# Attention with a gated feed-forward in one kernel: down products in one run per two sections, the activation and the gate reordered, fewer key transfers

## Chip, core and metric

The kernel runs on one core of a Trainium2 chip. The metric is the device time of one execution, in microseconds; the median of the runs is compared. TensorE multiplies matrices (PE in the profile, PEld is its weight load), VectorE is DVE, ScalarE is ACT, GpSimd is POOL, and SyncE (SP) issues the transfers.

## The reference

The input `x` has 2048 tokens of width 576. It is normalized once, and two branches read the result: attention with 32 heads of width 18, and a feed-forward of width 4608 with a gelu gate. The output joins them.

```python
def _A_ref(x, wqkv, wo):
    B, S, D = x.shape
    H = 32
    Dh = D // H
    qkv = (lambda x, *d: x.transpose(*d))((x @ wqkv).reshape(B, S, 3, H, Dh), 2, 0, 3, 1, 4)
    q, k, v = qkv[0], qkv[1], qkv[2]
    scores = jnp.einsum("bhqd,bhkd->bhqk", q, k) * (Dh ** -0.5)
    p = _softmax(scores, axis=-1)
    o = jnp.einsum("bhqk,bhkd->bhqd", p, v)
    return (lambda x, *d: x.transpose(*d))(o, 0, 2, 1, 3).reshape(B, S, D) @ wo

def _B_ref(x, w_gate, w_up, w_down):
    return (_gelu(x @ w_gate) * (x @ w_up)) @ w_down

x = A_x
xn = _layernorm(x, axis=-1)
s = _A_ref(xn, A_wqkv, A_wo)
g = _silu(_B_ref(xn, B_w_gate, B_w_up, B_w_down))
return x + s * g
```

## The kernel before, in words

Values are split into a high and a low part (`hi`, `lo`), and a product is made of three: high by high, high by low, low by high.

The prologue normalizes `x` by blocks of 512 tokens (`norm`), transposes it on TensorE (`transposes`, `pt`), makes queries and keys (`project`, `po`) and values (`values_of`), and stores all of it to DRAM (`qk`, `vs`, and `xhs` for the feed-forward). In the last block `split_wo` loads, splits and stores the output weights.

The main part is a sequence of 144 sections, counted from 0, that mix both branches. Four token blocks have 18 rounds each, and a round has two sections (G = 2). A section makes the gate and up sums `pg` and `pu` of 128 of the 4608 columns for 512 tokens: 27 pairs of products, each pair on the two halves of TensorE's rows. Among these pairs the program puts attention's products (`spread`): pairs of a score product `pe` (whose exponential ACT writes to `pT`) and a product `pm` of a later unit (whose row maximum DVE takes). The first nine sections (`FIRST` says how many pairs each takes) hold only products for maxima, sections 9 to 136 hold scores, the last seven none. After its pairs a section has, in this order, the values of attention (`values`, `acc`), the turn of a row of maxima (`max_end`, every fourth section), a projection by the output weights (`project_o`, `po`, in 8 sections per block, on dates that `at` writes down), and down products (`downs`, `py`). PE runs in program order; a scheduler orders the other engines' instructions, save those under `keep_in_program_order`.

`activate` makes gelu(`pg`) times `pu` from two operations on ACT and three on DVE; `pg` and `pu` have two banks together, so the next section's sums wait for the last reader. `finish` splits the result into `hh` and `hl`, and after a round's second section it splits the down weights `dh`, `dl` and queues the round's down products in two halves: token groups 0 and 1 in the next section, 2 and 3 in the one after. Each half is 24 products in four groups of six, and DVE adds each group to `Y` (it copies in round 0). In the last round of a block `down` then puts silu on `Y` at once, chunk by chunk of 128 by 288 values (`gate`: a tanh on ACT into the one buffer `th`, a DVE operation back into `Y`), and SP stores `Y` to `ys`. There are eight chunks at the end of each of the first three blocks, which falls in sections 36 and 37, 72 and 73, 108 and 109. `load_xy` reads a chunk back when its projection is due.

The banks of PSUM go by tags: `f` two (`pg`, `pu`), `s` two (`pe`, `py`), `m` three (`pm`, `po`), `acc` one. `load_k` and `load_q` fetch the 54 rows of a head (high, low, high for keys) in three transfers each; four heads are loaded for a chunk.

Of the kernel before, what the change touches and what calls it, by code (L numbers as in the profile page):

```python
# [8 lines left out]
F32 = mybir.dt.float32  # L9
# [8 lines left out]
P = 128  # L18
# [21 lines left out]
NF = NB * NR * G  # L40
FIRST = (0, 3, 5, 5, 5, 5, 5, 6, 6)
MROW = 3 * DH
HO = 7
# [8 lines left out]
def f(ap):  # L52
    return ap.bitcast(F32)
# [13 lines left out]
def kernel(ctx: ExitStack, tc: tile.TileContext, x, wqkv, wo, w_gate, w_up, w_down, out):  # L67
# [67 lines left out]
    with tc.tile_pool(name="pro", bufs=1) as pro, tc.tile_pool(name="pps", bufs=1, space=PSUM) as pps:  # L135
# [45 lines left out]
        def norm(xr, b, between=None):  # L181
# [21 lines left out]
            return last  # L203

        def transposes(b, xr):
            xt = XT[b % 2]
            pts = [pps.tile([P, TB], F32, name="pt", bufs=KT + 1) for k in range(KT + 1)]
            for j in range(4):
                for k in range(KT + 1):
                    nc.tensor.transpose(pts[k][:, j * P:(j + 1) * P], xr[j][:, k * P:(k + 1) * P], ident)  # L210
            for k in range(KT + 1):
                split_t(pts[k], k, xt)
            return xt
# [10 lines left out]
        for v in VN:  # L224
            nc.vector.memset(v, 1.0)
        ORDER = (4, 5, 0, 1, 6, 7, 8, 2, 3)
        WQK, WV = {}, {}
# [41 lines left out]
        def split_wo(k):  # L269
            n = min(KO, D - k * KO)  # L270
            raw = raw_tile([KO, D])
            tc.keep_in_program_order(nc.sync.dma_start(raw[0:n], wo[k * KO:k * KO + n, :]))
            hi, lo = (pro.tile([KO, D], F32R, name=f"wo{i}", tag="rawp", bufs=5) for i in range(2))
            split(hi[0:n], lo[0:n], raw[0:n])
            for i, t in enumerate((hi, lo)):
                nc.sync.dma_start(wos[i, k * KO:k * KO + n, :], f(t)[0:n])

# [21 lines left out]
        for b in range(NB):  # L299
            for n, t in enumerate(ORDER):  # L300
# [13 lines left out]
                if b == 0 and n in (7, 8):  # L314
                    split_wv(n - 7, raw_v[n - 7])
                project(b, t, xt)
                if b == NB - 1 and n < NK:
                    split_wo(n)
                if n == 4 and b + 1 < NB:
# [17 lines left out]

    FF = {"w": ahead, "xd": XD, "down": [], "n": 0}
    finals = []
# [16 lines left out]
    def gate(o, th, yy):  # L356

        nc.scalar.activation(th, yy, AF.Tanh, scale=0.5)
        nc.vector.scalar_tensor_tensor(o, th, 1.0, yy, op0=ALU.add, op1=ALU.mult)  # L359

    def activate(pg, pu):
        t1 = ffn.tile([P, TB], F32, name="t1", bufs=1)
        t2 = ffn.tile([P, TB], F32, name="t2", bufs=1)
        nc.scalar.activation(t1, pg, AF.Square)
        nc.vector.scalar_tensor_tensor(t2, t1, 1.0 / GC, pg, op0=ALU.add, op1=ALU.mult)  # L365
        nc.scalar.activation(t1, t2, AF.Tanh, scale=GC * GS)
        nc.vector.scalar_tensor_tensor(t2, t1, 1.0, pg, op0=ALU.add, op1=ALU.mult)
        nc.vector.scalar_tensor_tensor(t1, t2, 0.5, pu, op0=ALU.mult, op1=ALU.mult)  # L368
        return t1

    def down(b, r, hs, wd, Y, js):
# [18 lines left out]
        if b < NB - 1 and r == NR - 1:  # L390
            for j in js:
                t = b * 4 + j
                for c in range(2):
                    yy = Y[:, j, 288 * c:288 * c + 288]
                    gate(yy, ffn.tile([P, 288], F32, name="th"), yy)
                nc.sync.dma_start(ys[t * P:(t + 1) * P, :], Y[:, j, :])

    def section(specials=(), tag="f", raw_d=None, early=None):
# [6 lines left out]
        if g == 0:  # L405
            FF["hs"] = []
            if r == 0:
                FF["Y"] = ffn.tile([P, TB // P, D], F32, name="Y")
        keep = tc.keep_in_program_order if n == NU * NA + len(FIRST) + 1 else lambda i: i
# [22 lines left out]
    def finish(pool=ffn, cut=split, bufs=1):  # L432

        n = FF["n"] - 1
        b, r = divmod(n // G, NR)
        hh = ffn.tile([P, TB], F32R, name="hh", bufs=G + 1)
        hl = ffn.tile([P, TB], F32R, name="hl", bufs=G + 1)
        cut(hh, hl, FF["act"])
        FF["hs"].append((hh, hl))
        if n % G == G - 1:  # L440
            wd = FF.pop("wd", None)
            if not wd:
                wd = [pool.tile([P, G, D], F32R, name=m, bufs=bufs) for m in ("dh", "dl")]
                cut(*wd, FF["rawd"])
            for h in range(2):
                FF["down"].append((b, r, FF["hs"], wd, FF["Y"], (2 * h, 2 * h + 1), n + 1 + h))

# [53 lines left out]
    def project_o(b, i, S2=None, o=None):  # L501
# [10 lines left out]
        if b < NB - 1:  # L512
            nc.vector.scalar_tensor_tensor(yy, yy, 0.5, po[:, 0:288], op0=ALU.mult, op1=ALU.mult)
            nc.gpsimd.tensor_tensor(yy, yy, xx, op=ALU.add)
# [20 lines left out]
    for b in range(NB):  # L535
        last = b == NB - 1
        for k in range(NK):
            t0 = b * AB + max(-(-min(H, (k + 1) * HO) // QD) * NA + 3, 2 * NA + 10 + 3 * k)
            if not (last and k == NK - 1):
                at(t0, 0, load_o, b, k)  # L540
                at(t0 + 2 - last, 2, norm_o, k)
        first = (b + 1) * AB + 1 if last else max((b + 1) * AB + 6, (b + 1) * NR * G - len(FIRST) + 3)
        at(first - 2, 0, load_wo, 0)
        at(first - 1, 2, split_o, 0)
        for i in range(GROUPS):
            n = first + i
            if last and n >= ENDS - 1:
# [11 lines left out]
    with tc.tile_pool(name="att", bufs=1, reuse_waits="tile") as att:  # L559
# [7 lines left out]

        def load_k(n, keep=lambda i: i):

# [3 lines left out]
            cols = slice(c * TB, (c + 1) * TB)  # L573
            for r in range(2):
# [16 lines left out]

        def load_q(u):
            j, g = divmod(u, NQ)
            cols = slice(j * TB, (j + 1) * TB)
            for r in range(2):
                t = QS[u, r] = att.tile([P, TB], F32R, name=f"q{r}", bufs=3)
                for a in range(2):
                    q = f(t)[64 * a:64 * a + MROW, :]
                    h = QD * g + 2 * r + a
                    rows = slice(h * DH, (h + 1) * DH)  # L600
                    for n, i in enumerate((0, 0, 1)):
                        nc.sync.dma_start(q[n * DH:(n + 1) * DH, :], qk[i, rows, cols])

# [121 lines left out]
        for n in range(NU * NA):  # L725
# [22 lines left out]
    with tc.tile_pool(name="epi", bufs=1, reuse_waits="tile") as epi:  # L748
# [40 lines left out]
        for Y, j, c in finals:  # L789
# [6 lines left out]
            else:  # L796
                nc.vector.scalar_tensor_tensor(ss, th, 0.5, ss, op0=ALU.mult, op1=ALU.mult)
                put(ss, j, cc, nc.gpsimd)
        for i, o in zip(range(HIND + 1, GROUPS), os):
            th, ss, j, cc = late[i]  # L800
            po = project_o(NB - 1, i, o=o)
            nc.vector.scalar_tensor_tensor(ss, th, 0.5, po, op0=ALU.mult, op1=ALU.mult)
            put(ss, j, cc, nc.vector)
# [28 lines left out]
```

## Time and profile before

| | |
|---|---|
| median of 3 runs | 2670.77 us (2667.56 to 2672.83) |
| the profiled execution | 2674.07 us, of which the program's span is 2672.3 us |
| PE busy | 2648.8 us, 99% of the span |
| DVE busy | 2007.3 us, 75% |
| ACT busy | 1440.9 us, 54% |
| POOL busy | 1354.0 us, 51% |
| exponentials (`pT`, 128x512) | 2048, of 600 ns |
| row maxima (`mx`, 128x512) | 2048, of 686 ns |
| down products (`py`, 288 columns) | 3456, of 294 to 310 ns, overlapping |
| adds to `Y` (128x288) | 544, of 457 ns |
| the tanh of the gate (128x288) | 24 of 447 ns, and 8 in the last block |
| DMA | 121 GB/s on the mean, 44.8% of the 16 engines' time |

Products overlap in the pipeline, so a product's duration is longer than its step; what counts is the distance from one start to the next. A line of the timeline gives the start in the span, the time, engine, source line and operation, the tiles written and read, the shape and the count; in brackets stands the engine's idle time ahead of it and what ended it. Section numbers are counted on PE's products, and a section starts with its first `pg`.

### The profile page before, as it was taken

The page shows a single profiled execution, that of the slowest core. Times are in us where ns is not written, and L with a number is a line of the kernel's source. Part 1 is how long each engine was busy: PE and PEld are TensorE (multiplying, and loading weights), DVE is VectorE, ACT ScalarE, POOL GpSimd, SP SyncE. Part 2 cuts the span into 40 slices and gives each one's busy share as a digit, 9 for nine tenths or more (in the row PEclk, how much of TensorE's full clock was granted, in tenths as well). Part 3 has the DMA queues.
Part 4 walks back from the last instruction along what each step waited for, and adds up shares of the span by engine and source line. Part 5 has one row for each costly group of instructions (what it writes and reads, how often), then busy time and mean ns, then how long its engine had stood idle before and what let it go on. Part 6 is the DMA issues. An engine that isn't in the chain of part 4 may idle for free.

```text
span 2672.3 us, 55506 instructions
## 1 busy us (share of the span) xinstructions
PE 2648.8 (99%) x21000; PEld 2025.0 (76%) x21000; DVE 2007.3 (75%) x3432; ACT 1440.9 (54%) x2553; POOL 1354.0 (51%) x1439
## 2 busy tenths in 40 slices
PE   8999999999999999999999999999999999999999
PEld 7887777777777777777777777777777777777777
DVE  5327888888888877788888877788888877888445
ACT  3222466555666555566556655555666554666532
POOL 2117544544465555544456555554445556444563
PEclk9999999999999999999999999999999999999999
DMA  8866433344354334543346335433345454433341
GB/s 254 264 229 155 114 96 96 94 103 105 103 141 122 97 103 117 142 105 102 98 106 161 100 99 141 123 103 99 100 106 119 126 140 126 115 101 92 77 111 56
DMA packets 389143, 323.64 MB, mean 121 GB/s; under 512 B 105544, under 2 KB 302664, under 8 KB 388876
## 3 DMA queue, kind: packets, MB, share of 16 engines
q1 hardware_dynamic: 388876, 320.08, 44.8%
q8 instruction: 167, 2.74, 0.4%
q14 instruction: 100, 0.82, 0.1%
HBM read 266.58 MB, written 52.85 MB: 120 GB/s over the span
## 4 chain that ended last, share of the span: by engine, by line
PE 96%; DVE 2%; DMA 0%; ACT 0%; issue 0%; POOL 0%; SPq 0%; DVEq 0%
PE pg L351 27%; PE acc L673 17%; PE py L381 17%; PE pe L639 10%; PE pm L612 9%; PE pu L351 7%; PE po L156 7%; PE po L511 2%; DVE mx L613 1%; PE pt L210 0%; DVE Y L387 0%; DVE t L365 0%; DVE Y L359 0%; PE pm L622 0%; DMA xx<-in_A_x_dram 0%
## 5 line engine op out<-in xcount | busy, mean ns | idle before, releaser
L640 ACT ACTIVATE pT<-pe 128x512 f32<-128x512 f32 x2048 | 1165.3, 600 | 767.4 <-PE pm L612 610.7
L613 DVE TENSOR_REDUCE mx<-pm 128x1 f32<-128x512 f32 x2048 | 1295.2, 686 | 49.8 <-PE pm L612 29.2
L351 PE MATMUL pg<-xd,wh 64*128 64x512 f32 x2592 | 948.6, 398 | 0.5 <-issue 0.5
L351 PE MATMUL pu<-xd,wh 64*128 64x512 f32 x2592 | 946.5, 397 | 0.0
L639 PE MATMUL pe<-q,KS 56*128 56x512 f32 x2048 | 818.1, 407 | 0.1
L612 PE MATMUL pm<-KS,q 54*128 54x512 f32 x2048 | 799.5, 394 | 3.5 <-DVE mx L613 1.9
L91 POOL TENSOR_SCALAR wh<-raw 128x384 fp32r<-128x384 f32 x432 | 222.2, 515 | 882.6 <-DMA raw<-in_B_w_up_dram 516.0
L351 PEld LDWEIGHTS pg<-xd,wh 64*128 64x128 f32 x2592 | 483.3, 187 | 58.0 <-issue 22.6
L351 PE MATMUL pg<-xd,wl 64*128 64x512 f32 x1296 | 507.6, 392 | 0.0
L351 PE MATMUL pu<-xd,wl 64*128 64x512 f32 x1296 | 507.1, 391 | 0.0
L351 PEld LDWEIGHTS pu<-xd,wh 64*128 64x128 f32 x2592 | 483.6, 187 | 9.3 <-DVE t L368 1.4
L673 PE MATMUL acc<-pT,VS 128*32 128x512 f32 x4096 | 466.0, 595 | 0.0
L92 POOL TENSOR_TENSOR wl<-raw,wh 128x384 fp32r<-128x384 f32 x432 | 437.8, 1014 | 34.5
L639 PEld LDWEIGHTS pe<-q,KS 56*128 56x128 f32 x2048 | 369.3, 184 | 82.8 <-ACT pT L640 23.4
L612 PEld LDWEIGHTS pm<-KS,q 54*128 54x128 f32 x2048 | 377.2, 184 | 38.0 <-DVE mx L613 6.4
L387 DVE TENSOR_TENSOR Y<-py,Y 128x288 f32<-128x288 f32 x544 | 248.2, 457 | 203.5 <-PE py L381 202.6
L381 PE MATMUL py<-dh,hh 128*128 128x288 f32 x1152 | 357.6, 310 | 2.3 <-DVE Y L387 1.3
L381 PE MATMUL py<-dl,hh 128*128 128x288 f32 x1152 | 339.8, 295 | 0.0
L381 PE MATMUL py<-dh,hl 128*128 128x288 f32 x1152 | 338.5, 294 | 0.0
L673 PEld LDWEIGHTS acc<-pT,VS 128*32 128x32 f32 x4096 | 120.4, 109 | 275.8 <-issue 264.5
L381 PEld LDWEIGHTS py<-dh,hh 128*128 128x128 f32 x1152 | 216.0, 187 | 81.1 <-issue 41.1
L351 PEld LDWEIGHTS pg<-xd,wl 64*128 64x128 f32 x1296 | 242.1, 187 | 20.0
(110 smaller groups left out, 2811.6 us busy)
## 6 DMA issues: line engine op xcount, KB each, us to landing
KS<-qk SPq DMA_DIRECT2D x1536, 36.0 KB
raw<-in_B_w_gate_dram SPq DMA_DIRECT2D x144, 288.0 KB
raw<-in_B_w_up_dram SPq DMA_DIRECT2D x144, 288.0 KB
raw<-in_B_w_down_dram SPq DMA_DIRECT2D x68, 576.0 KB
VS<-vs SPq DMA_DIRECT2D x128, 152.0 KB
qk<-t SPq DMA_DIRECT2D x72, 256.0 KB
q<-qk SPq DMA_DIRECT2D x384, 36.0 KB
xd<-xhs SPq DMA_DIRECT2D x24, 384.0 KB
```

Source lines behind the costliest of these rows:

```text
L91: first = nc.gpsimd.tensor_scalar(hi, raw, 1.0, 1.0, op0=ALU.mult, op1=ALU.mult)
L92: nc.gpsimd.tensor_tensor(lo, raw, f(hi), op=ALU.subtract)
L156: nc.tensor.matmul(o, st, m, start=(i == 0), stop=(i == len(TERMS) - 1))
L351: nc.tensor.matmul(o, w[1 + wp][k][rr, c, :], xd[xp][k][rr, c, :], start=(i == 0), stop=(i == len(terms) - 1))
L381: nc.tensor.matmul(py, a[:, tt], w[:, g, cc], start=(n == 0), stop=(n == 3 * G - 1))
L387: nc.vector.tensor_tensor(yy, py, yy, op=ALU.add)
L511: nc.tensor.matmul(po[:, 0:288], o[x][0:n, k, :], OW[w][0:n, k, :], start=(m == 0), stop=(m == len(terms) - 1))
L612: nc.tensor.matmul(pm, QS[u, r][rr, t * P:(t + 1) * P], KS[(u * NA + c) % KB][r][rr, :], start=True, stop=True)
L613: nc.vector.tensor_reduce(MX[u][:, 2 * r + a, t, c:c + 1], pm, axis=AX.X, op=ALU.max)
L639: nc.tensor.matmul(pe, KS[(u * NA + c) % KB][r][rr, t * P:(t + 1) * P], QS[u, r][rr, :], start=True, stop=True)
L640: nc.scalar.activation(PT[u, kt][:, 2 * r + a, :], pe, AF.Exp, scale=SCALE)
L673: nc.tensor.matmul(ACC[u][32 * a:32 * a + 32, :], VS[(u * NA + c) % VB][:, v:v + 32], pt[:, a, :], start=(kt == 0), stop=(kt == NT - 1), s ...
```

## The change

`JOIN` names the sections whose rounds have all their down products in the section after the round, 48 in one run; the section after that has none. Projections of the first three blocks are dated two sections apart, in the sections that have the run. `activate` reads `pg` in three operations (square, DVE, a copy on ACT) and `pu` in one, on DVE, before the tanh; the factor 0.5 moves into the gate's scales. Silu of the first three blocks leaves `down`: `gates` runs one section later, with tanh on ACT, two operations on GpSimd and a store for each chunk, and `Y` is one tile for the whole run. 64 idle transposes of the identity are put ahead of the first transposes. Two rows of a head's three are loaded in one transfer, the first keys and queries are loaded by halves, the output weights' stores move two projections back, the lead sections get two empty places at the end, and some dates of `load_o` move.

```diff
+JOIN = (len(FIRST), len(FIRST) + NU * NA - G)
...
+        def warm(n):
+            o = pps.tile([P, TB], F32, name="po", bufs=3)
+            for i in range(n):
+                nc.tensor.transpose(o[:, 0:P], ident, ident)
...
+                if b == 0 and j == 0:
+                    warm(64)
...
+        def store_wo(k, n, hi, lo):
             for i, t in enumerate((hi, lo)):
-                nc.sync.dma_start(wos[i, k * KO:k * KO + n, :], f(t)[0:n])
+                tc.keep_in_program_order(nc.sync.dma_start(wos[i, k * KO:k * KO + n, :], f(t)[0:n]))
...
+                if b == NB - 1 and 2 <= n < NK + 2:
+                    store_wo(*parts.pop(0))
                 if b == NB - 1 and n < NK:
-                    split_wo(n)
+                    parts.append(split_wo(n))
...
     def gate(o, th, yy):
-        nc.scalar.activation(th, yy, AF.Tanh, scale=0.5)
+        nc.scalar.activation(th, yy, AF.Tanh, scale=0.25)
         nc.vector.scalar_tensor_tensor(o, th, 1.0, yy, op0=ALU.add, op1=ALU.mult)
 
     def activate(pg, pu):
         t1 = ffn.tile([P, TB], F32, name="t1", bufs=1)
         t2 = ffn.tile([P, TB], F32, name="t2", bufs=1)
         nc.scalar.activation(t1, pg, AF.Square)
-        nc.vector.scalar_tensor_tensor(t2, t1, 1.0 / GC, pg, op0=ALU.add, op1=ALU.mult)
-        nc.scalar.activation(t1, t2, AF.Tanh, scale=GC * GS)
-        nc.vector.scalar_tensor_tensor(t2, t1, 1.0, pg, op0=ALU.add, op1=ALU.mult)
-        nc.vector.scalar_tensor_tensor(t1, t2, 0.5, pu, op0=ALU.mult, op1=ALU.mult)
+        nc.vector.scalar_tensor_tensor(t1, t1, 1.0 / GC, pg, op0=ALU.add, op1=ALU.mult)
+        nc.scalar.activation(t2, pg, AF.Copy)
+        nc.vector.tensor_tensor(t2, t2, pu, op=ALU.mult)
+        nc.scalar.activation(t1, t1, AF.Tanh, scale=GC * GS)
+        nc.vector.scalar_tensor_tensor(t1, t1, 1.0, t2, op0=ALU.add, op1=ALU.mult)
         return t1
...
         if b < NB - 1 and r == NR - 1:
-            for j in js:
-                t = b * 4 + j
-                for c in range(2):
-                    yy = Y[:, j, 288 * c:288 * c + 288]
-                    gate(yy, ffn.tile([P, 288], F32, name="th"), yy)
-                nc.sync.dma_start(ys[t * P:(t + 1) * P, :], Y[:, j, :])
+            FF["gates"] += [(b, j, c, Y) for j in js for c in range(2)]
+
+    def gates():
+        for k, (b, j, c, Y) in enumerate(FF["gates"]):
+            rows, cc = slice(b * TB + j * P, b * TB + (j + 1) * P), slice(288 * c, 288 * c + 288)
+            if k < 3:
+                th = op.tile([P, 288], F32, name="th", tag=("yy", "yy", "xx")[k], bufs=(2, 2, 1)[k])
+            else:
+                th = ffn.tile([P, 288], F32, name="th")
+            tc.keep_in_program_order(nc.scalar.activation(th, Y[:, j, cc], AF.Tanh, scale=0.25))
+            nc.gpsimd.tensor_scalar(th, th, 1.0, 1.0, op0=ALU.add, op1=ALU.mult)
+            nc.gpsimd.tensor_tensor(th, th, Y[:, j, cc], op=ALU.mult)
+            nc.sync.dma_start(ys[rows, cc], th)
+        FF["gates"] = []
...
-                FF["down"].append((b, r, FF["hs"], wd, FF["Y"], (2 * h, 2 * h + 1), n + 1 + h))
+                once = JOIN[0] <= n < JOIN[1]
+                FF["down"].append((b, r, FF["hs"], wd, FF["Y"], (2 * h, 2 * h + 1), n + 1 + (0 if once else h)))
...
+        if not last:
+            first += (first + len(FIRST)) % G
...
-            n = first + i
+            n = first + i * (1 if last else G)
...
-                    for n_, i in enumerate((0, 1, 0)):
-                        keep(nc.sync.dma_start(kk[n_ * DH:(n_ + 1) * DH, :], qk[i, rows, cols]))
+                    keep(nc.sync.dma_start(kk[0:2 * DH, :], qk[:, rows, cols]))
+                    keep(nc.sync.dma_start(kk[2 * DH:MROW, :], qk[0, rows, cols]))
...
-        load_k(0)
-        load_q(0)
+        for r in range(2):
+            load_k(0, rs=(r,))
+            load_q(0, (r,))
...
-            section([lambda s=s: lead_pair(s) for s in range(slot, slot + m)], "s" if n == 1 else "f", lead_raw)
+            section([lambda s=s: lead_pair(s) for s in range(slot, slot + m)] + (m > 0) * 2 * [lambda: None],
+                    "s" if n == 1 else "f", lead_raw)
...
+            gates()
             tasks(n, 0)
```

More of the change, by code (lines that the diff above doesn't have):

```diff
@@ L225 @@
             nc.vector.memset(v, 1.0)
+        parts = []
         ORDER = (4, 5, 0, 1, 6, 7, 8, 2, 3)
@@ L274, in split_wo @@
             split(hi[0:n], lo[0:n], raw[0:n])
+            return k, n, hi, lo
+        def store_wo(k, n, hi, lo):
             for i, t in enumerate((hi, lo)):
-                nc.sync.dma_start(wos[i, k * KO:k * KO + n, :], f(t)[0:n])
+                tc.keep_in_program_order(nc.sync.dma_start(wos[i, k * KO:k * KO + n, :], f(t)[0:n]))
         NQT = 2 * D // P
@@ L335 @@
     ps = ctx.enter_context(tc.tile_pool(name="ps", bufs=1, space=PSUM))
-    FF = {"w": ahead, "xd": XD, "down": [], "n": 0}
+    FF = {"w": ahead, "xd": XD, "down": [], "gates": [], "n": 0,
+          "Y": ffn.tile([P, TB // P, D], F32, name="Y")}
     finals = []
@@ L406, in section @@
             FF["hs"] = []
-            if r == 0:
-                FF["Y"] = ffn.tile([P, TB // P, D], F32, name="Y")
         keep = tc.keep_in_program_order if n == NU * NA + len(FIRST) + 1 else lambda i: i
@@ L512, in project_o @@
         if b < NB - 1:
-            nc.vector.scalar_tensor_tensor(yy, yy, 0.5, po[:, 0:288], op0=ALU.mult, op1=ALU.mult)
+            nc.vector.scalar_tensor_tensor(yy, yy, 0.25, po[:, 0:288], op0=ALU.mult, op1=ALU.mult)
             nc.gpsimd.tensor_tensor(yy, yy, xx, op=ALU.add)
@@ L537 @@
         for k in range(NK):
-            t0 = b * AB + max(-(-min(H, (k + 1) * HO) // QD) * NA + 3, 2 * NA + 10 + 3 * k)
+            t0 = b * AB + max(-(-min(H, (k + 1) * HO) // QD) * NA + 3, 22 + 3 * k)
             if not (last and k == NK - 1):
@@ L566, with load_k @@
             nc.vector.memset(vv[:, VC * VW:], 0.0)
-        def load_k(n, keep=lambda i: i):
+        def load_k(n, keep=lambda i: i, rs=(0, 1)):
             u, c = divmod(n, NA)
@@ L573, in load_k @@
             cols = slice(c * TB, (c + 1) * TB)
-            for r in range(2):
+            for r in rs:
                 for a in range(2):
@@ L590, with load_q @@
         QS, MX, ACC, PT, NM, DEN = {}, {}, {}, {}, {}, {}
-        def load_q(u):
+        def load_q(u, rs=(0, 1)):
             j, g = divmod(u, NQ)
             cols = slice(j * TB, (j + 1) * TB)
-            for r in range(2):
+            for r in rs:
                 t = QS[u, r] = att.tile([P, TB], F32R, name=f"q{r}", bufs=3)
@@ L600, in load_q @@
                     rows = slice(h * DH, (h + 1) * DH)
-                    for n, i in enumerate((0, 0, 1)):
-                        nc.sync.dma_start(q[n * DH:(n + 1) * DH, :], qk[i, rows, cols])
+                    nc.sync.dma_start(q[0:DH, :], qk[0, rows, cols])
+                    nc.sync.dma_start(q[DH:MROW, :], qk[:, rows, cols])
         def max_mm(u, i, a):
@@ L796 @@
             else:
-                nc.vector.scalar_tensor_tensor(ss, th, 0.5, ss, op0=ALU.mult, op1=ALU.mult)
+                nc.vector.scalar_tensor_tensor(ss, th, 0.25, ss, op0=ALU.mult, op1=ALU.mult)
                 put(ss, j, cc, nc.gpsimd)
@@ L801 @@
             po = project_o(NB - 1, i, o=o)
-            nc.vector.scalar_tensor_tensor(ss, th, 0.5, po, op0=ALU.mult, op1=ALU.mult)
+            nc.vector.scalar_tensor_tensor(ss, th, 0.25, po, op0=ALU.mult, op1=ALU.mult)
             put(ss, j, cc, nc.vector)
```

## The prediction

> **What bounds the kernel now.** I read the page first, its engine line and the chain that ended last:
>
> ```profile
> PE 2648.8 (99%) x21000; PEld 2025.0 (76%) x21000; DVE 2007.3 (75%) x3432; ACT 1440.9 (54%) x2553; POOL 1354.0 (51%) x1439
> ...
> PE 96%; DVE 2%; DMA 0%; ACT 0%; issue 0%; POOL 0%; SPq 0%; DVEq 0%
> ```
>
> TensorE sets the end. Its work is not cut (the change adds 64 small transposes), so only the steps between its products, and what makes it wait, can move the time. Next, the timeline of PE where one of the 128 long sections passes into the next:
>
> ```profile
> 400.81 0.61 PE L673 MATMUL acc<-pT,VS 128*32 128x512 f32 x4
> 401.35 0.40 PE L381 MATMUL py<-dh,hh 128*128 128x288 f32 x1
> 401.59 0.30 PE L381 MATMUL py<-dl,hh 128*128 128x288 f32 x1
> 401.72 0.29 PE L381 MATMUL py<-dh,hl 128*128 128x288 f32 x1
> ...
> 404.53 0.29 PE L381 MATMUL py<-dh,hl 128*128 128x288 f32 x1
> 404.76 0.49 PE L351 MATMUL pg<-xd,wh 64*128 64x512 f32 x1
> 404.76 0.49 PE L351 MATMUL pu<-xd,wh 64*128 64x512 f32 x1
> 405.09 0.39 PE L639 MATMUL pe<-q,KS 56*128 56x512 f32 x1
> ...
> 405.32 0.40 PE L351 MATMUL pg<-xd,wl 64*128 64x512 f32 x1
> ```
>
> A section is three blocks by start times: 43 pairs of gate/up, score and max products (10.38 us), the values `acc` (3.57), and 24 down products `py` (3.41). A change of kind costs a little: into `py`, 0.54 from the last group of four `acc` against 0.43 between groups, then 0.24 to the second product against 0.13; out, 0.23 against 0.13, then 0.33 to the second pair against 0.23.
>
> Third, ACT inside the 43 pairs, first an ordinary section, then the one from 805.95, after a token block's end:
>
> ```profile
> 405.52 10.09 ACT L640 ACTIVATE pT<-pe 128x512 f32<-128x512 f32 x16 [5.39 <-PE pm L612]
> ```
> ```profile
> 806.53 0.45 ACT L358 ACTIVATE th<-Y 128x288 f32<-128x288 f32 x1 [0.79 <-DVE Y L359]
> 806.88 0.59 ACT L640 ACTIVATE pT<-pe 128x512 f32<-128x512 f32 x1
> 808.00 0.45 ACT L358 ACTIVATE th<-Y 128x288 f32<-128x288 f32 x1 [0.53 <-DVE Y L359]
> 808.35 2.27 ACT L640 ACTIVATE pT<-pe 128x512 f32<-128x512 f32 x4
> ```
>
> Sixteen exponentials fill 10.09 of the 10.38 us, and `pe` has two banks: PE can be two ahead, no more. One tanh that waited 0.53 us among them made the 43 pairs 11.53 us instead of 10.38. So what ACT loses inside the pairs, PE loses. This decides the forecast.
>
> **Part by part.**
>
> *Downs in one run.* After the change, sections alternate: one ends with 48 `py`, the next goes from `acc` straight to `pg`; 63 runs of 24 vanish. In a run a product steps by (404.53-401.59)/22 = 0.134 us, so 24 appended ones cost 3.21 against 3.41: 0.20 saved, 63 x 0.20 = -12.6 us. The switch `acc` to `pg` is not in this trace. If it costs nothing, 0.41 is saved per run (-26); if it costs as much as the two that it replaces, 0. I take one switch, as all four rows above cost 0.10 to 0.11 a step.
>
> *Evictions and activation in the short section.* Vector adds 0.46 us per group of six products that take 0.80; 48 in a run do not change that. In a short section sums must be free 3.6 us after the last pair. Square (0.60) and copy (about 0.60) run on ACT after the last exponential, to about 1.7; the vector operations on the two sums end by about 2.4. Covered. Uncovered, the 144 added copies would be 86 us. GpSimd and the queue have at least as long per pair of sections as before.
>
> *Projections* move to every second section, those with `py`; their 15 products and the 0.13 step into `py` stay: 0.
>
> *Silu taken out of the down section.* The six sections after block ends (37, 38, 73, 74, 109, 110) have 10.98, 11.53, 11.59, 11.51, 11.46, 11.49 us of pairs, together 6.3 over 10.38: -6.3.
>
> *Silu put late.* The order of the changed program has, at each of three block ends, ACT do four tanh in the short section's `acc` block, then in the long section's pairs: 4 exponentials, tanh, 3, tanh, 2, tanh, 3, tanh, 4. Chunks 0 to 2 have buffers of their own; the other five share the one `th`. Now GpSimd finishes a chunk in place and SP stores it, so each of the last four tanh waits until the store before it has landed, and the exponentials queue behind it.
> GpSimd reaches the first chunk after two weight splits, which end 3.2 us behind the last pair (415.27 to 418.4), about when the next pairs begin. A chunk is 0.43 (scaled from the 0.515 of 384 columns and 0.623 of 512) plus 0.80 (the `yy` row); with hand-overs, chunk 3 is done 5.3 us into the pairs. By the semaphores in the trace, the 24 stores of this size (`out<-yy`) landed 1.75 to 4.33 us after issue, median 2.22. So tanh 4 starts at about 7.6, where four exponentials are through at 3.3. A link is 0.45 + 0.43 + 0.80 + 2.22 + 0.15 = 4.05: tanh 7 starts at 7.6 + 3 x 4.05 = 19.8, and with itself and four exponentials the last ends at 22.7 instead of 10.85. That is 11.9 us, three times: +35.6. With stores at 1.75 and GpSimd 0.7 sooner it is 28; with a slow store behind the 576 KB `w_down` load, 45.
>
> *The start.* The first 20 transposes begin at 10.91, at 0.213 us a step, and pass to 0.109 after 3.4 us; at 45.37 twenty take 2.1. The 64 idle ones can start at 1.3 (identity ready): 16 x 0.213 + 48 x 0.109 = 8.6, done by 10. The last rows are normalized at 12.5; the first copy out then starts at 13.0 instead of 14.60: -1.6. If all 64 ran at the slow step they would end at 15: +2.
>
> *First keys and lead sections.* PE waits 1.7 us for the first queries:
>
> ```profile
> PE pm L612 <- DMA q<-qk: 1.7, 2, 1.3
> ```
>
> SP issues 24 small loads one after another at some 0.33 us; 16 remain and the first half suffices. In the lead sections `pu` waits about 0.4 us for the last vector operation on it, which now comes before the tanh (seven sections, about -2.9). Against that, max products that stand closer (two empty places at the end) meet three banks and 0.67 us per reduction: +0.3 to +1 a section. Net -2.0, between -5 and +3. Joint key loads later and the moved `wo` stores: 0, no wait of PE names them.
>
> *The tail.* Five sections have one `py` step of 0.47 to 0.49 instead of 0.24 for a late eviction; the activation ends 0.7 us sooner: -1.2.
>
> **Sum:** -12.6 - 6.3 - 1.6 - 2.0 - 1.2 + 35.6 = +11.9. The profiled execution took 2674.07 us (span 2672.3), so 2686.0 like for like; it lay 3.3 above the median of 2670.77, so 2682.7 for the median.
>
> A rule that speaks against it: nothing in this trace shows what a long stop of PE does to its clock; after 1.5 us of waiting at 209.35 the pairs still step at 0.23. The Trainium skill's page "TensorE: Matmul & The Clock Gate" (What's actually happening) says that an idle window of some 3.4 us halves the clock until about 3.4 us of work has passed. By that, an estimate from the page, the longest stop at each block end could add up to 1.7 us, 5 in all, and the sum would be 2688.
>
> **Rivals.**
> *The waits are covered (faster).* If GpSimd got to the chunks early and stores landed while exponentials ran, only the four tanh themselves would cost: 3 x 4 x 0.45 = 5.4, so -18.3: 2652.5. For it: the scheduler spaced them by two to four exponentials, as if that were enough. Against: three exponentials are 1.9 us, and a landing alone is 2.22. It decides if a link is under 2.5 us. Chance 0.16.
> *Half of it.* Links of 3 us, or a tanh that finds its buffer free: stall near 24, sum 0, 2671. Chance 0.16.
> *The direct switch costs as much as the old two.* `acc` to `pg` changes both row and column split. Then -12.6 falls away: 2695. For it: untried here; against: each step seen costs 0.10 to 0.11, whichever kinds meet. Chance 0.08.
> *Long runs stall on evictions.* The last section's run of 48 took 7.48 us against 6.62 here; 0.86 x 63 = 54, 2737. Against: there vector also activated and gated between the adds, here it is through before the run. Chance 0.04.
> The forecast keeps 0.56.
>
> **How the numbers follow.** 2682.7 is the likeliest case. Its own range, from the stall (28 to 45) and the start, is 2672 to 2696. Range: 2660 to 2698 takes in the half case, the costlier switch and the near part of the covered one; the run of 54 and most of the covered case stay out. About 0.2% (5.3 us) is what a measurement here can tell from no change. Slower by more: 0.66 (the forecast but a few hundredths, and the two dear rivals); within: 0.18 (the half case and that edge); faster: 0.16.
>
> **What would show it.** Right: in the sections after 36, 72 and 108 the pairs take 20 us or more, ACT's waits name the store `ys<-th` in front of tanh, twelve times about 2 to 4 us; ordinary pairs of sections take 34.5 instead of 34.7; the first projections start at 13.6 instead of 15.25. Wrong: no DMA wait on ACT, or pairs of 12 us there; a step of over 0.6 from `acc` to `pg`; runs of 48 `py` over 7 us; transposes of 0.213 after 10.9.

## The result: 3% slower, and the profile after

The changed kernel takes 2751.77 us (median of 4 runs, 2750.09 to 2752.47) where the kernel before takes 2669.42 (4 runs, 2667.56 to 2672.83): a ratio of 1.0305, 95% interval 1.0291 to 1.0319. The forecast was 2682.7 with a range to 2698: the sign was right, the size was not. The profiled execution has a span of 2750.7 us against 2672.3, so 78.4 us more.

First the chain that ended last, shares by engine, in the profile after:

```profile
PE 91%; DMA 4%; POOL 2%; DVE 1%; ACT 1%; issue 0%; SPq 0%; POOLq 0%; ACTq 0%
```

Before, PE had 96% of it and DMA 0%. Transfers now stand in the path. Then the waits after (who waited for whom: us in total, times, longest):

```profile
ACT th L419 <- DMA ys<-th: 49.7, 12, 14.0
...
PE pe L668 <- ACT pT L669: 42.2, 9, 14.0
...
PE pu L367 <- POOL xd L127: 15.7, 15, 2.6
```

The first two rows are the forecast's stall: twelve waits of tanh for a store, and TensorE behind the exponentials that stand behind them, but of up to 14.0 us where 2 to 4 were forecast. The third was in no step of the forecast: the first gate and up products of a block wait for their input tiles `xd`.

The ordinary sections did what was forecast. The timeline of PE after, at a section without down products:

```profile
914.31 1.47 PE L702 MATMUL acc<-pT,VS 128*32 128x512 f32 x12
915.71 0.50 PE L367 MATMUL pg<-xd,wh 64*128 64x512 f32 x1
...
916.05 0.39 PE L668 MATMUL pe<-q,KS 56*128 56x512 f32 x1
```

`acc` passes straight to `pg` with one ordinary switch (0.52 us, as into `py`) and no wait, a run of 48 takes 6.62 us, and a pair of sections takes 34.49 us instead of 34.72. So neither the rival of a dear switch nor that of stalled runs came.

Taking PE's section starts from both traces, the 78.4 us lie here. The row of sections 0 to 2 is the stretch that the expectations below call section 2; "pairs" is the part of a section ahead of its first `acc`.

| place | before | after | difference |
|---|---|---|---|
| start of section 0 (the prologue) | 199.79 | 197.94 | -1.9 |
| sections 0 to 2 (the first attention products) | 28.35 | 40.97 | +12.6 |
| section 4 | 11.76 | 17.03 | +5.3 |
| pairs of sections 36, 72, 108 together | 31.1 | 57.9 | +26.8 |
| pairs of sections 37, 73, 109 together | 34.0 | 31.1 | -2.9 |
| pairs of sections 38, 74, 110 together | 34.5 | 84.7 | +50.2 |
| sections 137 to 140 | 46.5 | 47.9 | +1.4 |
| everything else (the runs of 48 above all) | | | -13.0 |

### The profile page after: what moved, and what is told of

It reads as the page before. It is cut to its first block, busy times and chain, and to the rows that moved or that the text cites. A ratio compares the mean times of both kernels' runs of the same rounds, so it can differ in the third digit from the quotient of the medians.

```text
span 2750.7 us, 55310 instructions
## 1 busy us (share of the span) xinstructions
PE 2669.2 (97%) x21064; PEld 2058.6 (75%) x21064; DVE 2004.4 (73%) x3408; ACT 1507.9 (55%) x2697; POOL 1396.5 (51%) x1487
## 4 chain that ended last, share of the span: by engine, by line
PE 91%; DMA 4%; POOL 2%; DVE 1%; ACT 1%; issue 0%; SPq 0%; POOLq 0%; ACTq 0%
PE pg L367 25%; PE py L399 17%; PE acc L702 16%; PE pe L668 9%; PE pm L641 8%; PE pu L367 7%; PE po L157 6%; PE po L537 2%; DMA xd<-xhs 1%; DMA KS<-qk 1%; DMA ys<-th 1%; PE po L210 0%; POOL th L421 0%; POOL xd L127 0%; PE pt L219 0%
## 5 line engine op out<-in xcount | busy, mean ns | idle before, releaser
L367 PE MATMUL pu<-xd,wh 64*128 64x512 f32 x2592 | 959.4, 402 | 15.7 <-POOL xd L127 15.7
L367 PE MATMUL pg<-xd,wh 64*128 64x512 f32 x2592 | 958.8, 401 | 0.9 <-issue 0.5
L367 PE MATMUL pg<-xd,wl 64*128 64x512 f32 x1296 | 513.2, 396 | 0.0
```

The source lines that it names most:

```text
L367: nc.tensor.matmul(o, w[1 + wp][k][rr, c, :], xd[xp][k][rr, c, :], start=(i == 0), stop=(i == len(terms) - 1))
```

## The experiments

Each run stands beside runs of the kernel before on its own chip (medians of 2669.07 to 2671.97 us); ratios are against those. Where two runs come from different chips, the difference of their bare medians is good to some 3 us, and the ratios are the better guide. Two theories were on the table at first. T: the joint loads of keys and queries are slow and make other transfers late. S: the short section in front of a block's end takes the cover from something there.

**Single transfers again, in the changed kernel (sep).**

```diff
-                    keep(nc.sync.dma_start(kk[0:2 * DH, :], qk[:, rows, cols]))
-                    keep(nc.sync.dma_start(kk[2 * DH:MROW, :], qk[0, rows, cols]))
+                    for n_, i in enumerate((0, 1, 0)):
+                        keep(nc.sync.dma_start(kk[n_ * DH:(n_ + 1) * DH, :], qk[i, rows, cols]))
```
(and the queries likewise)

> The changed kernel with keys and queries fetched in three transfers a head, as before; all else as changed. Theory T (transfers): the two-row transfers land late (in the changed trace 5.6 us at the median against 2.05 for the single ones before) and hold up SP and all that lands behind them; then section 2 falls from 41.0 to some 28 us, section 4 from 17.0 to 11.4, the pairs of sections 36, 72, 108 from 18.6 to 20.1 down to 10.4, and those of 38, 74, 110 from 26 to 31 down to about 22, as the chain of stores alone was priced: 2685 to 2692 us. Rival S (short section): the block ends stall since section 35, 71, 107 end 3.4 us sooner and the next block's activations come no faster; then 36, 72, 108 stay near 19 us, and only the start recovers: 2715 to 2735 us.

Measured: 2712.06 us (2708.77 to 2713.89), ratio 1.0158 (1.0142 to 1.0173). The joint transfers cost the changed kernel 39.7 us. Sections 0 to 2 went back to 28.60 and section 4 to 11.32; the pairs of section 38 fell from 30.90 to 21.92. Those of section 36 stayed at 18.15. So the time lies between the two ranges, just under S's, and the 39.7 us are T's: both theories hold a part.

**The joint transfers alone, in the kernel before (joint_alone).** The reverse edit.

> The kernel before with the two-row transfers alone. Theory T: it loses what the start lost (some 18 us in sections 2 and 4) and perhaps some at the block ends, where 6.6 us more of down products give the reload time: 2685 to 2710 us. Rival S: no loss at the block ends and a few microseconds at most at the start, since SP has fewer transfers to issue: 2666 to 2676 us.

Measured: 2701.13 us (2698.41 to 2703.15), ratio 1.0117 (1.0102 to 1.0132). Nothing else of the change is needed for a loss of 31 us. Sections 0 to 2 alone take 41.21 us instead of 28.35. Waits of PE and ACT between 199 and 242 us of this run:

```profile
PE pm L612 <- DVE mx L613: 6.5, 1, 6.5
...
PE pm L612 <- DMA q<-qk: 4.3, 2, 3.6
```
```profile
ACT dh L96 <- DMA pT<-in_B_w_down_dram: 11.0, 1, 11.0
```

Before, the queries held PE for 1.7 us there. The first row names VectorE, but its reductions stood behind the activation, and that stood behind ACT's cut of the down weights (last row): their load was issued behind the key loads at 217.18 us, 2 us later than before, and landed after 7.5 us instead of 4.9. Other transfers are late in the whole of this run: the value tiles `VS` land after 5.44 us at the median, 2.51 before. And PE worked 17.0 us at a granted clock of 0.50 after such stops, before none; a pair of products then steps by 0.43 us instead of 0.23, so that is, as an estimate, up to 8 of the 31 us.

**Silu back in the down section (joint_oldgate, sep_oldgate).** The first keeps the joint transfers, the second has single ones.

```diff
-            FF["gates"] += [(b, j, c, Y) for j in js for c in range(2)]
+            for j in js:
+                for c in range(2):
+                    yy = Y[:, j, 288 * c:288 * c + 288]
+                    gate(yy, ffn.tile([P, 288], F32, name="th"), yy)
+                nc.sync.dma_start(ys[t * P:(t + 1) * P, :], Y[:, j, :])
```

> The changed kernel with silu put back into down, on VectorE and into Y, with one store for two chunks; the two-row transfers stay. Both theories: the pairs of 38, 74, 110 fall to 10.4 to 12 us, as no store stands before a tanh. Theory T: start (41 us) and 36, 72, 108 (about 19 us) stay as they are: 2698 to 2708 us. A third theory, that the late silu itself delays the reload at the block ends, would bring 36, 72, 108 back to 10.4 as well: 2672 to 2680 us.

Measured: 2716.48 us (2711.41 to 2718.75), ratio 1.0173 (1.0158 to 1.0188): slower than either theory said. Beside the next run, the joint transfers cost 20.3 us here, against 39.7 with the late silu: the two make each other dearer.

> The changed kernel with both undone, three transfers a head and silu in down on VectorE. What stays: runs of 48, the new activation, 64 idle transposes, halves of the first keys, two empty places. Theory T: faster than before by the 12.6 us of the runs, 1.6 of the transposes and 1 to 4 of start and tail, with 2 to 6 us lost around the block ends: 2652 to 2660 us. Rival S: 36, 72, 108 stay near 19 us: 2678 to 2685 us.

Measured: 2696.22 us (2695.8 to 2697.65), ratio 1.0099 (1.0082 to 1.0116). With both suspects gone 26 us are still lost, so neither theory was complete. The trace says where: sections 35 and 36 together take 43.58, 43.35 and 43.95 us at the three block ends, against 34.9 before. There the tiles `xd` of the next block are reloaded. The queue of SP, first in the kernel before, where section 36 starts at 770.65, then in run sep, where it starts at 763.97:

```profile
756.24 2.42 SPq L125 DMA_DIRECT2D xd<-xhs  x2
```
```profile
755.36 1.26 SPq L126 DMA_DIRECT2D xd<-xhs  x2
```

The first reload is issued 14.4 us ahead of the section that needs it before, and 8.6 us ahead after. Of the 5.8 us lost, 3.4 are the 24 products that section 35 no longer has. The rest is seen on GpSimd, in the kernel before and in run sep:

```profile
761.08 1.46 POOL L126 CAST xd<-xd 64x1536 fp32r<-64x1536 f32 x1 [2.70 <-DMA xd<-xhs]
```
```profile
751.25 2.68 POOL L93 TENSOR_TENSOR dl<-raw,dh 128x1152 fp32r<-128x1152 f32 x1
...
762.56 1.46 POOL L127 CAST xd<-xd 64x1536 fp32r<-64x1536 f32 x1 [7.06 <-DMA xd<-xhs]
```

GpSimd prepares the first tile 9.6 us ahead of section 36 before, and 1.4 us ahead in sep. The cut of the next down weights can start only when the run of 48 has let go of the old ones (749.8), the gate and up splits come after it, and the `raw` buffer that they free is what SP waits for ahead of the `xd` loads. In the order of SP's queue this makes the second reason; it was read from the trace, and not tried on its own.

**The last two runs of each block split again (sep_oldgate_edge).**

```diff
-                once = JOIN[0] <= n < JOIN[1]
+                once = JOIN[0] <= n < JOIN[1] and r < NR - 2
```

> The changed kernel with single key and query transfers, silu in the down run, and the last two runs of each block (sections 34/35 and 36/37 of a block's round) split into two of 24 as before. Theory S (without its 24 products section 35 no longer covers the reload of the 6 input tiles xd, 8.4 to 9.0 us at each of three block ends): the 26 us and the 8.7 us of two sections' silu in one go away, 2658 to 2664. Rival R (the reload is late for another reason, such as the order of POOL's or SP's work in the changed activation): 2686 to 2697.

Measured: 2663.7 us (2661.35 to 2664.69), ratio 0.997 (0.9958 to 0.9982). Sections 35 and 36 take 34.91, 35.07 and 34.96 us. GpSimd has the first tile 10.2 us ahead of section 36 (764.48) again:

```profile
754.30 1.47 POOL L127 CAST xd<-xd 64x1536 fp32r<-64x1536 f32 x1 [2.10 <-DMA xd<-xhs]
```

S is shown: 25.9 us of loss came from a section 35 with nothing behind its `acc` (in the changed kernel itself, these sections stand 26.7 us above the kernel before). How much of it is the missing cover and how much GpSimd's order, no run separates.

**What the late silu waits for (sep_inplace, sep_inplace_edge, dvegate_edge).** The first writes the last step into `Y` and stores from there, so that the buffer `th` is free when GpSimd has read it, not when a store has landed. In these expectations T stands for another theory, that the landings of the stores set the pace.

```diff
-            nc.gpsimd.tensor_tensor(th, th, Y[:, j, cc], op=ALU.mult)
-            nc.sync.dma_start(ys[rows, cc], th)
+            nc.gpsimd.tensor_tensor(Y[:, j, cc], th, Y[:, j, cc], op=ALU.mult)
+            nc.sync.dma_start(ys[rows, cc], Y[:, j, cc])
```

> The changed kernel with single key and query transfers, and the last silu step written into Y, from which the store goes, so that the next tanh waits for GpSimd's read of th and not for a store's landing. Theory T (the tanh waits for landings cost 11.7, 14.0 and 12.6 us at the three block ends): 2670 to 2680. Rival G (GpSimd's two steps, late behind its cuts, set the tanh as well): 2690 to 2712.

Measured: 2711.31 us (2708.14 to 2712.22), ratio 1.0147 (1.0132 to 1.0162), no different from sep. Taking away the landing changed the name of the wait and little else: the pairs of sections 38, 74 and 110 take 20.57, 21.04 and 21.13 us, in sep 21.92, 22.76 and 22.39. ACT's waits ahead of tanh, run sep, then run sep_inplace:

```profile
ACT th L419 <- DMA ys<-th: 29.4, 11, 4.4
```
```profile
ACT th L419 <- POOL Y L421: 22.7, 12, 3.4
```

> As the in-place kernel, and the run before the last of each block split into two of 24, so that section 35 keeps 24 products. Theories T and S together: 2642 to 2656, below the kernel before. T alone true: 2668 to 2680. S alone true: 2662 to 2686. Neither: 2690 or more.

Here only the run before the last of a block is split (`r != NR - 2`). Measured: 2689.19 us (2686.81 to 2690.22), ratio 1.0064 (1.0047 to 1.008): 22 us better by the split, as S says; the theory of landings fails again.

The third takes GpSimd out of the chain:

```diff
-            nc.gpsimd.tensor_scalar(th, th, 1.0, 1.0, op0=ALU.add, op1=ALU.mult)
-            nc.gpsimd.tensor_tensor(Y[:, j, cc], th, Y[:, j, cc], op=ALU.mult)
+            nc.vector.scalar_tensor_tensor(Y[:, j, cc], th, 1.0, Y[:, j, cc], op0=ALU.add, op1=ALU.mult)
```

> As the in-place kernel with a split run before each block's end (2689.2), and the late silu's last two steps on GpSimd made one step on VectorE. Theory G (GpSimd's queue and its two steps of 0.43 and 0.80 us set the tanh chain, 10 us a block end): 2660 to 2670. Rival (ScalarE, with 16 exponentials of 0.6 us in 10.4 us of pairs, has no room for eight tanh of 0.45 us there, or VectorE's row maxima take GpSimd's place): 2676 to 2690.

Measured: 2669.73 us (2667.7 to 2674.45), ratio 1.0002 (0.9992 to 1.0011). The waits of tanh that are left in this run:

```profile
ACT th L419 <- DVE Y L420: 7.1, 6, 1.9
```

GpSimd's queue and its two steps were worth some 17 us by the ratios (19.5 by bare medians). Sections 37 and 38 still take 39.42 us here against 34.5 for an ordinary pair: the tanh and the steps on VectorE have a price among the 16 exponentials and maxima, as the rival said. Both were part of it.

**Joined runs without, and with, the new reading of the sums (join_edge_warm, act_alone, join_edge_warm_act).** All three start from the kernel before. The first adds the runs of 48 (but for the last two of a block), the projection dates, some dates of `load_o`, and the idle transposes.

```diff
+                once = JOIN[0] <= n < JOIN[1] and r < NR - 2
-                FF["down"].append((b, r, FF["hs"], wd, FF["Y"], (2 * h, 2 * h + 1), n + 1 + h))
+                FF["down"].append((b, r, FF["hs"], wd, FF["Y"], (2 * h, 2 * h + 1), n + 1 + (0 if once else h)))
```

> The kernel before with runs of 48 every second section, except the last two runs of each block, and the 64 idle transposes; transfers, silu and the sums' operations as before. By the prediction's own terms 57 joined runs x 0.20 and 1.6: 2656 to 2660. Rival (a run of 48 in itself makes later work wait, as GpSimd's cut of the next down weights comes after it): 2668 or more.

Measured: 2676.47 us (2674.86 to 2678.84), ratio 1.0018 (1.0008 to 1.0027): slower by 4.5 us, where the forecast's own terms gave 13 us of gain. A short section returns to the pairs while VectorE still reads the old sums. VectorE and PE of this run:

```profile
876.22 0.69 DVE L377 SCALAR_TENSOR_TENSOR t<-t,pu 128x512 f32<-128x512 f32 x1
```
```profile
876.60 0.49 PE L360 MATMUL pg<-xd,wh 64*128 64x512 f32 x1
876.97 0.50 PE L360 MATMUL pu<-xd,wh 64*128 64x512 f32 x1
```

`pu` starts 0.37 us behind `pg`, just after the vector operation on its bank ends at 876.91. In the short sections of this run it lags 0.17 and 0.36 us in turn; elsewhere the two start together. The second run has the new reading of the sums alone:

```diff
-        nc.vector.scalar_tensor_tensor(t2, t1, 1.0 / GC, pg, op0=ALU.add, op1=ALU.mult)
-        nc.scalar.activation(t1, t2, AF.Tanh, scale=GC * GS)
-        nc.vector.scalar_tensor_tensor(t2, t1, 1.0, pg, op0=ALU.add, op1=ALU.mult)
-        nc.vector.scalar_tensor_tensor(t1, t2, 0.5, pu, op0=ALU.mult, op1=ALU.mult)
+        nc.vector.scalar_tensor_tensor(t1, t1, 1.0 / GC, pg, op0=ALU.add, op1=ALU.mult)
+        nc.scalar.activation(t2, pg, AF.Copy)
+        nc.vector.tensor_tensor(t2, t2, pu, op=ALU.mult)
+        nc.scalar.activation(t1, t1, AF.Tanh, scale=GC * GS)
+        nc.vector.scalar_tensor_tensor(t1, t1, 1.0, t2, op0=ALU.add, op1=ALU.mult)
```

> The kernel before with the three-operation reading of the gate and up sums alone. Theory A (it matters only where a section has no products behind it: the old chain frees the sums 3.9 us after the last pair, against a rest of 6.97 us in every section before): 2667 to 2674, no change. Rival (it frees ScalarE and VectorE for the exponentials in every section): 2655 to 2664.

Measured: 2672.29 us (2669.64 to 2674.26), ratio 1.0007 (0.9998 to 1.0016): no change. The third has both:

> The joined runs and idle transposes of the run that gave 2676.5, with the three-operation reading of the sums added. Theory A (a section without products returns to the pairs after 3.57 us, and the old chain, 3.9 us, holds the first pair's sum): the joined pairs of sections go from 0.08 slower than before to 0.17 faster, 57 x 0.25 = 14 us: 2660 to 2666. Rival (order of the lead sections' work and loads made the gain of the run at 2663.7): 2672 to 2678.

Measured: 2660.91 us (2660.46 to 2663.27), ratio 0.9967 (0.9954 to 0.998). VectorE and PE at the same place:

```profile
872.26 0.69 DVE L377 TENSOR_TENSOR t<-t,pu 128x512 f32<-128x512 f32 x1 [0.66 <-ACT t L376]
```
```profile
873.50 0.49 PE L360 MATMUL pu<-xd,wh 64*128 64x512 f32 x1
```

The sum is free at 872.95, 0.55 us before PE wants it. By the ratios, the new reading is worth 13.6 us on top of the joined runs (15.6 by bare medians) and nothing without them. This kernel and sep_oldgate_edge (ratio 0.997) are the fastest, level within their intervals: the part of the change that pays, without the part that doesn't.

**Why the joint transfers are slow (keys_two_halves, rows_by_2, rows_by_9).** In the trace a transfer's landing is a set of updates to its semaphore. A single key load, 18 rows, has ten; a joint one, two by 18 rows, has three. The first attempt wrote the source of the single load as two halves:

```diff
-keep(nc.sync.dma_start(kk[n_ * DH:(n_ + 1) * DH, :], qk[i, rows, cols]))
+keep(nc.sync.dma_start(kk[n_ * DH:(n_ + 1) * DH, :], qk[i, rows, cols].rearrange('(a d) t -> a d t', a=2)))
```

> The kernel before, in which each single key transfer of 18 rows is written as two halves of 9 rows in its source; bytes, transfers and issue count as before. Theory K (the number of DMA engines that a transfer gets follows the outermost size, 2 for the two-row transfers and 9 for single ones, so that the key loads queue on two engines): 2695 to 2730, with three completion updates for each key transfer as in the joint ones. Rival I (the joint transfers cost by their 0.6 us issue or by being fewer and larger): 2666 to 2676, and ten updates.

Measured: 2669.03 us (2667.53 to 2671.54), ratio 0.9997 (0.9988 to 1.0007), and ten updates a transfer as before. Two adjoining halves are still one even pattern, so this run tested nothing. The next two took the rows in an order that can't be joined, alike in keys and queries (`'(d a) t -> a d t'` with a=2, then with a=9):

> The kernel before; each single key and query transfer of 18 rows takes its source rows in the order 0, 2, 4 ... 1, 3, 5 ... (outermost size 2, inner 9), alike in keys and queries, so that the products are the same. Transfers, bytes and rows as before. Theory K (the outermost size sets how many DMA engines share a transfer, two here as in the two-row transfers, which had three completion updates each): three updates a transfer, and 1.5 times the bytes that the joint loads put on two engines: 2695 to 2750. Rival I (issue time or larger transfers): 2666 to 2676.

Measured: 2825.47 us (2822.65 to 2828.66), ratio 1.0587 (1.0572 to 1.0603). Slower than K's range. Three updates a transfer, median landing 5.82 us (2.05 before), and `VS` lands after 5.62 us.

> As the run by 2, with the source rows in the order 0, 9, 1, 10 ... (outermost size 9, inner 2): a pattern just as broken up, and nine engines by theory K: ten updates, 2666 to 2676. If the broken pattern itself costs, it is as slow as the run by 2.

Measured: 2720.27 us (2714.85 to 2722.61), ratio 1.0196 (1.0179 to 1.0213). Ten updates and a median landing of 2.30 us (`VS` 2.46), as K says, yet 51 us slower, which K did not say. SP's rows on the key loads tell why (nanoseconds least, median and most of one issue), in the kernel before, joint_alone, rows_by_2 and rows_by_9:

```profile
L580 SPq DMA_DIRECT2D KS<-qk x1536: 263/312/1782, 200.6 to 2455.5; - x192
```
```profile
L579 SPq DMA_DIRECT2D KS<-qk x512: 586/630/2405, 200.0 to 2482.0; - x171
```
```profile
L580 SPq DMA_DIRECT2D KS<-qk x1536: 580/588/2476, 201.0 to 2614.1; - x192
```
```profile
L580 SPq DMA_DIRECT2D KS<-qk x1536: 724/728/1380, 201.2 to 2500.9; - x192
```

Two costs, then. A source of two levels takes SP about twice as long to issue (0.588 and 0.728 us against 0.312). Where every key and query load has one, in rows_by_9, the run loses 51 us; its landings are hardly later, so the issues are what is left, but no run tried them alone. And a pattern whose outermost size is 2 lands late: rows_by_2 issues a little faster than rows_by_9 and loses 105 us more. In the joint kernel the first cost is small, since two transfers of 0.630 and 0.426 us take the place of three of 0.312 (1.06 against 0.94 us a head); that its losses come mostly from the second is argued from this. The start of joint_alone agrees: the two-row loads are issued some 1.2 us apart (200.01, 201.27, 202.50, 203.63 us) and land 1.62 us apart (204.35, 205.98, 207.59, 209.21 us), 73.7 KB in 1.62 us or 45 GB/s, where single loads land every 0.3 to 0.4 us.

The records of single packets show how many move at once. In rows_by_2, between 204.5 and 214 us, two are under way for 7.8 of the 9.5 us and never fewer. In rows_by_9 it is up to ten, and none for 4.3 us, when SP has issued no more.

The Trainium skill's page "DMA: Bandwidth & Descriptors" (Why a DMA increments its semaphore by 16 and not by 1) has the rule: a transfer goes to the largest number of engines up to 16 that divides the outermost size of both sides, and the semaphore gets one update for the remainder at once and one from each engine. By it 18 rows use nine engines and two by 18 rows use two. The updates here agree: ten and three, and sixteen for the 128 rows of `VS`. The same page says that such a transfer uses the lowest-numbered engines, so always the same two; no view of these runs shows an engine's number, but that `VS`, with its sixteen updates, lands late beside the two-row loads fits it.

## Why the prediction failed, step by step

*Downs in one run, -12.6:* right in the changed kernel; a pair of sections is 34.49 where 34.5 was forecast. But the reason given for pricing the activation at 0 ("Covered") hid what it does: with the old one the run's gain is gone (join_edge_warm). The two edits are one.

*Silu out of the down section, -6.3:* as forecast in the pairs of sections 37, 73 and 109, which fell to 10.36; sections 38, 74 and 110 have the late silu now.

*Idle transposes, -1.6:* -1.9; the first projections start at 13.69 us (13.6 forecast).

*The tail, -1.2:* +1.4 in sections 137 to 140 and -0.5 in the last. A small miss whose cause is open.

*Silu put late, +35.6:* in the kernel with single transfers, sections 37 and 38, 73 and 74, 109 and 110 took 46.17, 48.51 and 47.08 us against 34.5 for an ordinary pair: 38.3. The size was right, and the chain came out link by link. ACT in sep, where the pairs begin at 806.92:

```profile
814.10 0.44 ACT L419 ACTIVATE th<-Y 128x288 f32<-128x288 f32 x1 [4.42 <-DMA ys<-th]
```
```profile
818.05 0.44 ACT L419 ACTIVATE th<-Y 128x288 f32<-128x288 f32 x1 [1.06 <-DMA ys<-th]
```

Tanh 4 starts 7.2 us into the pairs and tanh 7, at 827.20, 20.3 us into them, where 7.6 and 19.8 were forecast; a link is 4.4 us against 4.05, with landings of 2.00 to 3.06. The mechanism was half right all the same: the landing was part of the link, but without it GpSimd held tanh nearly as long (sep_inplace), which the forecast did not see. In the changed kernel, with joint transfers, the term is 54.8 us by the same count, and the pairs alone grew by 50: the first of the four tanh waits was 13.96 us, because GpSimd came to the chunks late. The timeline of GpSimd and of ACT, after:

```profile
830.51 0.51 POOL L92 TENSOR_SCALAR wh<-raw 128x384 fp32r<-128x384 f32 x1 [7.09 <-DMA raw<-in_B_w_up_dram]
...
833.62 0.83 POOL L420 TENSOR_SCALAR th<-th 128x288 f32<-128x288 f32 x2
```
```profile
826.71 2.46 ACT L669 ACTIVATE pT<-pe 128x512 f32<-128x512 f32 x4 [0.23 <-PE pm L641]
843.13 0.44 ACT L419 ACTIVATE th<-Y 128x288 f32<-128x288 f32 x1 [13.96 <-DMA ys<-th]
```

The pairs begin at 825.88. The forecast had GpSimd start about there, as the pairs begin; a late load of `w_up` (7.60 us from issue to landing) made it 7.7 us later, and the first four stores took 3.87 to 5.41 us to land, the fourth at 843.05.

*"Joint key loads later ...: 0, no wait of PE names them":* **the failed step**, 39.7 us of the 69.1 by which the forecast of 2682.7 was short. It read the waits of before, where the loads had 0.3 us issues and ten updates, as a property of the loads and not of their shape. The same slip made "First keys and lead sections" -2.0 instead of +17.9 in sections 0 to 2 and 4: "the first half suffices" is of no use when the first half's two-row loads land more than 1.4 us apart. With single loads (sep), sections 0 to 8 take 0.8 us less than before.

*"GpSimd and the queue have at least as long per pair of sections as before":* **the second failed step**, 25.9 us, which with the first makes 65.6. True of a pair of sections on the mean; but at a block's end a given load has to land in a given section, and that one lost the 24 products that had covered it. No rival priced this; the nearest row, the `xd` loads of 4.3 to 10.5 us, was in the trace.

One path from the changed kernel back has four steps: 39.7 for the transfers, 15.8 for the late silu over the old one in the same joined run (2712.06 less 2696.22), 32.5 for the split at the block ends (`xd`, and the old silu in one section instead of two), and what is left of the change, 5.7 faster than before (2669.42 less 2663.7; 8.3 against the runs on its own chip). They add up to the 82.35 measured (2751.77 less 2669.42) because each starts where the last one ends, and the shares depend on the order: with the late silu taken out first, it is worth 35.3 and the transfers 20.3.

## What to carry to other kernels

Before merging transfers to save issues, look at the outermost size of the new pattern and count the completion updates of the old one: fewer, larger transfers can land later, and make others late. When work is moved out of a section, list what that section covered for others, load by load, at the places where the rhythm breaks (block ends, first sections), not on the mean. And test an edit together with the one that makes it possible: the joined runs lost 4.5 us alone, the early-freed sums gained nothing alone, and together they gained 9.

## What the runs showed of the chip that was not expected

A stopped TensorE comes back at half clock. Stretches of the changed kernel (busy times of PE, PEld, DVE, ACT and POOL, granted clock, DMA share, GB/s), after the stop of 14.3 us that ended at 844.11:

```profile
849.00:850.00 1.00, 1.00 (x8) 1.00 (x6) 0.15 (x2) 0.00 (x0) 0.00 (x0) 0.50 0.93 348
850.00:851.00 1.00, 0.54 (x5) 0.10 (x1) 1.00 (x2) 0.03 (x1) 0.00 (x0) 1.00 0.05 16
```

The clock record of this run falls to 0.50 at 832.94, 2.8 us into the stop, and returns to 1.00 at 850.00, 5.9 us after PE resumed, with steps of 0.43 us a pair instead of 0.23 meanwhile. In sep, after a stop of 4.2 us (810.92 to 815.08), it was 0.50 from 814.15 to 820.98. That bears out the rule of the Trainium skill that the prediction weighed ("TensorE: Matmul & The Clock Gate", What's actually happening) in kind; the way back took nearly 6 us here, with short waits in it, against some 3.4 us of work on the page.

The low stretches last 3.41, 6.83, 10.24 or 17.07 us, multiples of 3.41. Cut into such pieces, the records of nine runs show that PE was busy for 60% at most of the piece ahead of each fall, and for 85% or more of the piece ahead of each return; pieces with 46 to 60% went either way. So a stop of 1.84 us was enough in sep (822.20 to 824.04, clock at 0.50 from 824.39), where the prediction had seen only a stop of 1.5 us, without effect. After its prologue the changed kernel worked 47.7 us at half clock, against none before. The 5 us that the prediction weighed for this are too few for that; as an estimate from the steps, up to 22 us, but much of it lies under the tanh chain, which PE waited for in any case.

A row order of two levels about doubled the issue time of a load on SP, from 0.31 to between 0.59 and 0.73 us, for the same bytes and rows.
